# First batch of an attention kernel: softmax rows left unscaled, columns scaled after the value product

## Chip, cores and metric

The kernel runs on one core of one Trainium2 chip. The metric is device time in microseconds of one execution, as the median of several runs. The engines are TensorE (PE, with its weight loads PEld), VectorE (DVE), ScalarE (ACT), GpSimd (POOL) and SyncE (SP), which issues all DMA transfers of this kernel.

## The reference, cut to what matters

Attention with a memory part, over B = 4 batches, H = 8 heads, S = 576 tokens, D = 64, followed by two gated layers:

```python
a = np.exp(scores - scores.max(-1, keepdims=True))      # causal, scale 1/sqrt(D)
a /= a.sum(-1, keepdims=True) + 1e-09
local = np.matmul(a, v)
mem_out = (phi(q) @ M_prev) / (phi(q) @ z_prev + 1e-06)  # per row
g = 1.0 / (1.0 + np.exp(-beta))                          # per head
attn = g * mem_out + (1 - g) * local
x = attn as (2304, 512)
x = (sigmoid(x @ w_gate) * (x @ w_val)) @ w_out          # first layer, d_ff 1536
x = (h * clip(h + 3, 0, 6) / 6) @ w_out2, h = x @ w_in   # second layer, d_ff 2048
```

All of it is float32. In attention the products are float32 matmuls; in the layers each operand is split into a high and a low part and a product is three matmuls.

## The kernel before, in words

The program has three phases. Phase A does attention and, between its pieces, the first six of twelve feature blocks of the first layer; B does the rest of the first layer, C the second. Only A bears on the change.

Attention goes in 32 **visits** (`VISITS`, numbered v = 0 to 31). One visit is a pair of heads of one batch and one of two ranges of query rows: `rg` 0 is the first 320 tokens, `rg` 1 the other 256. The order is by batch, so visits 0 to 3 (`rg` 0) and 4 to 7 (`rg` 1) are the first batch. A visit takes two steps t of the loop in `phase_a`.

In a visit, TensorE makes scores (tile `s`, L344). DVE takes them from PSUM, adds the mask, writes them to tile `P` and keeps each row's minimum of the negated score (`m`, the custom instruction of L324; a row's first pass covers up to 320 or 448 columns, and for long rows a second pass of 256 or less). ACT takes the exponential in place and sums each row into `l` (L362). `normalize` then makes 1 / ((l + 1e-9) (1 + e^beta)) on DVE (L385, L386) and multiplies each row of `P` by it, on ACT (L390) in steps 5 to 26 and for the longest rows, else on DVE (L392). The first 64 columns of each row of `P` hold the memory part, phi(q) times `nr`, which `memory_rows` puts there on POOL (L377); `nr` comes from `prep_phi` (L297 to L309), which starts from the tile `aux` that a DMA brings. Three steps later TensorE transposes `P` in banks of four blocks (tile `t`, L402), ACT copies them to SBUF (`T`, L404), and `pv` multiplies by the memory matrix and the values (L426), ACT copies the product to `xpr` (L435), and SP stores it to DRAM (L438 to L442).

While the attention runs, weights of the layers are loaded as 64-bit values (`wst`, two 512 KB transfers each, L142) and **converted** by ACT and DVE to high and low halves: ACT L152, DVE L153, L154, L155, then ACT L163 and DVE L157, L158, L164. Nine such conversions of two blocks each lie in the first 117 us; the tile `wst` has two buffers, so a load waits for the conversion two before it. The first layer's matmuls (`m`, L233 to L235) come in between attention's pieces as soon as a stretch of 312 tokens has its attention; the first of them stand behind the value product of visit 4.

TensorE's order is the order in which the code is written (`manual_schedule`). The orders of DVE, ACT, POOL and SP are set by the scheduler of the framework, when the program is built, by its own estimate of times; each engine then works through its list in that order. PSUM tiles: `s` and `m` share four buffers (`ps_m`, tag `m`), `t` has three, `pv` one. The tile `aux` has three buffers, so the load for visit v + 3 waits for the value product of visit v.

Of the kernel before, what the change touches and what calls it, by code (L numbers as in the profile page):

```python
# [8 lines left out]
F32 = mybir.dt.float32  # L9
# [4 lines left out]
ALU = mybir.AluOpType  # L14
# [16 lines left out]
RANGES = [(0, 1, 2), (3, 4)]  # L31
# [15 lines left out]
NW_A = 3 * NFA // 2  # L47
NW_B = 3 * (FF1 - NFA) // 2
NLATE = 2

FILL = (5, 9, 8, 9, 8, 8)

# [26 lines left out]
class Kernel:  # L79
# [232 lines left out]
    def new_weights(self, v, rg):  # L312
        vs, nb = self.visits[v], len(ROWS[rg])
        vs["P", rg] = self.pa2.tile([128, 2304], F32, name="P", tag="P", bufs=3)
        vs["l", rg] = self.pa2.tile([128, 5], F32, name="l", tag="l")[:, :nb]
        vs["m", rg] = self.pa2.tile([128, 5], F32, name="m", tag="m")[:, :nb]

    def row(self, v, rg, r, a, e):
# [58 lines left out]
        self.nc.gpsimd.tensor_tensor(out, ph, nr, op=ALU.mult)  # L377

    def normalize(self, v, rg, act):
        nc = self.nc  # L380
        pr = self.visits[v]
        h = pr["pair"][1]
        l, nb = pr["l", rg], len(ROWS[rg])
        c0 = 5 * (h // 2) + 5 - nb
        nc.vector.scalar_tensor_tensor(l, l, 1e-9, self.a1[:, c0 : c0 + nb], op0=ALU.add, op1=ALU.mult)  # L385
        nc.vector.reciprocal(l, l)  # L386
        for r in range(nb):
            a = self.row(v, rg, r, 64, row_at(rg, r)[1])
            if act or row_at(rg, r)[1] == 640:
                nc.scalar.activation(a, a, AF.Copy, scale=l[:, r : r + 1])  # L390
            else:
                nc.vector.tensor_scalar_mul(a, a, l[:, r : r + 1])  # L392

    def transpose_bank(self, v, rg, k):
        nc = self.nc
        pr = self.visits[v]
        if k == 0:
            pr["T", rg] = self.pa2.tile([128, 2304], F32, name="T", tag="T")
        ps = self.ps_t.tile([128, 512], F32, name="t", tag="t")
        bank = BANKS[rg][k]  # L400
        for n, (r, j) in enumerate(bank):
            nc.tensor.transpose(ps[:, 128 * n : 128 * n + 128], self.row(v, rg, r, 128 * j, 128 * j + 128), self.ident)  # L402
        c = 128 * len(bank)
        nc.scalar.copy(pr["T", rg][:, 512 * k : 512 * k + c], ps[:, :c])  # L404

    def pv(self, v, rg):
        nc = self.nc
        pr = self.visits[v]
        b, h = pr["pair"]
        t0, nt = RTOK[rg]  # L410
        ps = self.ps_v.tile([128, 512], F32, name="pv", tag="pv")
        ops, T = [], pr["T", rg]
        for g in range(2):
            if rg == 0:

                o = 64 * g
                mine = [(0, 0, 320 * g, 320), (1, o, 640 + 256 * g, 256), (2, o + 128, 1152 + 128 * g, 128)]
            else:
                mine = [(j, 0, 1152 * g + 256 * j, 256) for j in range(4)] + [(4, 128, 1152 * g + 1024, 128)]
            ops.append(mine)  # L420
        last = len(ops[0]) - 1
        for n in range(last + 1):
            for g in range(2):
                j, o, c, w = ops[g][n]
                rows = slice(64 * g, 64 * g + 64)
                nc.tensor.matmul(  # L426
                    ps[rows, o : o + w],
                    pr["v"][:, j, rows],
                    T[:, c : c + w],
                    start=(n == 0),  # L430
                    stop=(n == last),
                    skip_group_check=True,
                )
        x = self.pa2.tile([128, 320], F32, name="xpr", tag="xpr")
        nc.scalar.copy(x[:, :nt], ps[:, :nt])  # L435
        dst = self.xd[h // 2, :, b * S + t0 : b * S + t0 + nt]
        if rg == 0:
            nc.sync.dma_start(dst[64:], x[64:, :nt])  # L438
            nc.sync.dma_start(dst[:64, 64:], x[:64, : nt - 64])
            nc.sync.dma_start(dst[:64, :64], x[:64, nt - 64 : nt])  # L440
        else:
            nc.sync.dma_start(dst, x[:, :nt])  # L442
        if h == H - 2:
            self.done[b, rg] = self.step
# [63 lines left out]
    def phase_a(self):  # L508
        nc, tc = self.nc, self.tc
# [8 lines left out]
        nt = len(steps)  # L518
        self.xnext = None
        stream, c = None, 0  # L520
# [30 lines left out]
        t = self.step = 0  # L551
# [5 lines left out]
        while t < nt or tq or vq:  # L557
            self.step = t
            fill = FILL[max(c - 1, 0)]
            first = w = 0  # L560
            if t < nt:
                v, rg, i = steps[t]
                if i == UNITS[rg][0][-1]:
                    self.new_weights(v, rg)
                w = 64 + 128 * i
                first = w if w <= 512 else 320
                self.score_part(v, i, 0, first)
            if t == 0:
                self.prep_phi(0)
            if t < nt and i == RANGES[rg][-1]:  # L570
                self.memory_rows(v, rg)
            transposes(t, 2)
            if vq and vq[0][0] <= t:
                self.pv(*vq.pop(0)[1])
            if first < w or (tq and tq[0][0] <= t):
                moe(fill // 2)
                fill -= fill // 2
                if first < w:
                    self.score_part(v, i, first, w)
                transposes(t, 1)  # L580
            if t < nt:
                self.exponentials(v, i)
                if i == RANGES[rg][-1]:
                    self.normalize(v, rg, 5 <= t < 27)
                    tq += [(t + 3, (v, rg, j)) for j in range(len(BANKS[rg]))]
            moe(fill)
            if t < nt and i == UNITS[rg][0][-1]:
                self.load_visit(v + 2)
            if t < nt and i == RANGES[rg][-1]:
                self.prep_phi(v + 1)  # L590
            if t >= 5 and t % 2:
                self.w_convert()
            if len(self.wstaged) < 2:
                self.w_load()
            t += 1
# [6 lines left out]
        self.bx = self.pool(ctx, "bx", 1)  # L602
        self.wpool2 = self.pool(ctx, "wslots2", NW_B - NLATE)
        self.ps_g = self.pool(ctx, "ps_g", 4, space=PSUM)
# [6 lines left out]
        self.plan_weights(keys, [])  # L611
        self.wpools = [self.wpool2] * (NW_B - NLATE)
        for _ in range(2):
            self.w_load()
        n = 0
        while c < NCA or stream is not None:
            self.step += 1
            moe(8)
            if n < NW_B - NLATE - 2:
                self.w_next()  # L620
# [4 lines left out]
        self.br = self.pool(self.b_ctx, "br", 1, side="right")  # L625
        self.wpool3 = self.pool(self.b_ctx, "wslots3", NLATE)
        self.wpools += [self.wpool3] * NLATE + [self.wpool] * 2 * NPAIR
        self.ps_a = self.pool(ctx, "ps_a", 4, space=PSUM)
# [345 lines left out]
```

## Time and profile before

| | before |
|---|---|
| median of 3 runs | 1067.75 us (1067.61 to 1069.07) |
| the profiled execution: its time | 1067.68 us |
| the profiled execution: span in the trace | 1065.9 us |
| PE busy | 1029.6 us (97%) |
| DVE busy | 645.5 us (61%) |
| ACT busy | 550.8 us (52%) |
| POOL busy | 83.5 us (8%) |

The time is 1.8 us more than the span: what lies around it. Shares are of the whole span; the first 80 us, in which the first layer has no work yet, look quite different from the rest. TensorE's granted clock is 0.997 of full speed on the mean.

### The profile page before, as it was taken

How to read it: one execution, taken by the hardware profiler on the slowest of the kernel's cores; microseconds unless marked ns; L12 is line 12 of the kernel's file. 1: busy time of each engine (PE TensorE's matmuls, PEld its weight loads, DVE VectorE, ACT ScalarE, POOL GpSimd, SP SyncE). 2: the span in 40 equal slices, each digit the busy share in tenths (PEclk: the TensorE clock that was granted, in tenths of full speed). 3: DMA queues.
4: the chain of work that ended last, by engine and by line, in shares of the span. 5: the costliest groups of instructions: out<-in, count | busy, mean ns of one | idle time of the engine just before them, and what ended most of it. 6: DMA issues, size and time to landing. Idle time of an engine off the chain costs nothing.

```text
span 1065.9 us, 16031 instructions
## 1 busy us (share of the span) xinstructions
PE 1029.6 (97%) x5824; PEld 886.0 (83%) x5824; DVE 645.5 (61%) x1543; ACT 550.8 (52%) x1191; POOL 83.5 (8%) x102
## 2 busy tenths in 40 slices
PE   5689999999999999999999999999999999999998
PEld 3367678878887899999888888888888888888886
DVE  6989755454455438888888888743454433643432
ACT  5999875576556644435444343433453333633432
POOL 3212211110111000000000000310002000000000
PEclk9999999999999999999999999999999999999999
DMA  7756542424242215336686877444404542044511
GB/s 227 215 177 198 189 126 75 137 80 123 68 125 79 62 47 179 119 119 250 231 295 246 310 261 275 152 158 188 148 30 158 217 155 103 10 164 172 218 40 60
DMA packets 66239, 164.87 MB, mean 155 GB/s; under 512 B 8432, under 2 KB 41712, under 8 KB 60272
## 3 DMA queue, kind: packets, MB, share of 16 engines
q1 hardware_dynamic: 66160, 163.85, 44.8%
q8 instruction: 46, 0.75, 0.3%
q14 instruction: 33, 0.27, 0.1%
HBM read 122.76 MB, written 41.06 MB: 154 GB/s over the span
## 4 chain that ended last, share of the span: by engine, by line
PE 84%; DVE 5%; ACT 5%; DMA 4%; issue 1%; SPq 1%; POOL 1%; ACTq 0%; POOLq 0%; DVEq 0%
PE acc L822 18%; PE pa L787 9%; PE pb L787 7%; PE m L233 6%; PE m L234 5%; PE m L235 5%; PE g L235 5%; PE g L233 5%; PE g L234 5%; PE pv L426 4%; PE t L402 4%; PE s L344 3%; PE acc L234 2%; PE acc L235 2%; PE acc L233 2%; DMA aux<-in_aux 1%
## 5 line engine op out<-in xcount | busy, mean ns | idle before, releaser
L822 PE MATMUL acc<-wslot,hs 128*128 128x512 f32 x864 | 227.8, 395 | 2.2 <-ACT hs L228 2.2
L822 PEld LDWEIGHTS acc<-wslot,hs 128*128 128x128 f32 x864 | 159.5, 188 | 27.7 <-ACT hs L228 3.5
L787 PE MATMUL pa<-xq,wslot 128*128 128x384 f32 x576 | 117.3, 338 | 1.1 <-ACT u L887 0.6
L787 PEld LDWEIGHTS pa<-xq,wslot 128*128 128x128 f32 x576 | 103.7, 187 | 9.9 <-ACT u L887 0.9
L235 PE MATMUL g<-xs,wslot 128*128 128x468 f32 (+1 forms) x288 | 106.4, 370 | 0.0
L234 PE MATMUL g<-xs,wslot 128*128 128x468 f32 (+1 forms) x288 | 106.2, 369 | 0.0
L233 PE MATMUL g<-xs,wslot 128*128 128x468 f32 (+1 forms) x288 | 104.1, 369 | 0.0
L362 ACT ACTIVATE P<-P,m 128x192 f32<-128x192 f32 (+4 forms) x144 | 83.9, 584 | 31.1 <-DVE m L324 29.8
L233 PE MATMUL m<-xs,wslot 128*128 128x312 f32 x288 | 93.8, 326 | 0.3 <-DVE m L324 0.3
L234 PE MATMUL m<-xs,wslot 128*128 128x312 f32 x288 | 88.1, 306 | 0.0
L235 PE MATMUL m<-xs,wslot 128*128 128x312 f32 x288 | 87.9, 305 | 0.0
L787 PE MATMUL pb<-xq,wslot 128*128 128x384 f32 x432 | 87.8, 338 | 0.0
L787 PEld LDWEIGHTS pb<-xq,wslot 128*128 128x128 f32 x432 | 77.9, 188 | 6.3
L344 PE MATMUL s<-qk 64*128 64x320 f32 (+3 forms) x320 | 67.9, 494 | 13.6 <-DMA qk<-in_qk 10.8
L851 DVE TENSOR_TENSOR c<-pb,u 128x384 f32<-128x384 f32 x48 | 26.6, 555 | 87.0 <-ACT u L887 86.0
L799 ACT ACTIVATE r<-c,three 128x384 f32<-128x384 f32 x72 | 44.2, 613 | 63.0 <-DVE c L851 63.0
L402 PEld LDWEIGHTS t<-ident,P 128*128 128x128 f32 x464 | 52.8, 143 | 25.1 <-issue 14.9
L402 PE MATMUL t<-ident,P 128*128 128x128 f32 x464 | 67.2, 281 | 5.6 <-ACT T L404 2.7
L229 DVE TENSOR_TENSOR hs<-r,hs 128x384 fp32r<-128x384 f32 x96 | 55.8, 585 | 26.8 <-ACT hs L228 25.4
L324 DVE CUSTOM_DVE_ANT_0 P<-s,mask 128x320 f32<-128x320 f32 (+3 forms) x144 | 62.5, 452 | 12.9 <-PE s L344 12.5
L404 ACT COPY T<-t 128x512 f32<-128x512 f32 (+2 forms) x128 | 65.6, 540 | 8.8 <-PE t L402 8.7
L426 PE MATMUL pv<-T,aux 128*64 128x256 f32 (+2 forms) x512 | 61.3, 367 | 8.3 <-ACT T L404 8.3
(101 smaller groups left out, 1918.4 us busy)
## 6 DMA issues: line engine op xcount, KB each, us to landing
wst<-in_wm SPq DMA_DIRECT2D x68, 512.0 KB, 5.7
wslot<-wd SPq DMA_DIRECT2D x30, 1024.0 KB, 5.1
wd<-wslot SPq DMA_DIRECT2D x16, 1024.0 KB, 4.8
wslot<-wd SPq DMA_DIRECT2D x15, 768.0 KB, 6.2
wd<-wslot SPq DMA_DIRECT2D x8, 768.0 KB, 5.6
qk<-in_qk SPq DMA_DIRECT2D x32, 160.0 KB, 2.4
aux<-in_aux SPq DMA_DIRECT2D x16, 320.0 KB, 3.3
qk<-in_qk SPq DMA_DIRECT2D x16, 288.0 KB, 3.0
```

The costliest lines, as they stand in the source:

```text
L229: elo.tensor_tensor(lo, src, hi.bitcast(F32), op=ALU.subtract)
L233: nc.tensor.matmul(out, w[0], x[0], start=first, stop=False)
L234: nc.tensor.matmul(out, w[0], x[1], start=False, stop=False)
L235: nc.tensor.matmul(out, w[1], x[0], start=False, stop=last)
L324: self.nc.vector.tensor_tensor_reduce(out=self.row(v, rg, r, 64 + a, 64 + e), in0=ps, in1=mask, scale=-0.125, scalar=3.0e38 if a == 0 else ...
L344: nc.tensor.matmul(ps[:, : e - a], qk[rows, 0, q0 : q0 + 128], qk[rows, 1, a:e], start=True, stop=True)
L362: self.nc.scalar.activation(x, x, AF.Exp, bias=vs["m", rg][:, r : r + 1], scale=-1.0, accum_out=vs["l", rg][:, r : r + 1])
L402: nc.tensor.transpose(ps[:, 128 * n : 128 * n + 128], self.row(v, rg, r, 128 * j, 128 * j + 128), self.ident)
L404: nc.scalar.copy(pr["T", rg][:, 512 * k : 512 * k + c], ps[:, :c])
L426: nc.tensor.matmul(ps[rows, o : o + w], pr["v"][:, j, rows], T[:, c : c + w], start=(n == 0), stop=(n == last), skip_group_check=True,)
L787: nc.tensor.matmul(ps[:, :HC], w[:, i, b, cc], x[:, l, k], start=first and k == 0 and n == 0, stop=last and k == 1 and n == 2, skip_group_ ...
L822: nc.tensor.matmul(a, h[:, i, cc], w[:, l, f], start=first and f == 0 and n == 0, stop=last and f == 1 and n == 2)
```

## The change

For visits 0 to 7 (`POST = 8`), `normalize` no longer scales the rows of `P`. With f = (l + 1e-9)(1 + e^beta) for a row, it multiplies `nr` by f, so that the memory columns of `P` carry the same factor as the unscaled exponentials, and makes 1 / f. `memory_rows` is called after `normalize` for these visits, since it needs the new `nr`; before, it stood behind the scores. Behind the value product, `spread` turns 1 / f, which lies over partitions, into a PSUM tile `rl` with the factors along columns, the same in all 64 partitions of a head: a matmul of `l`'s column, repeated 64 times, with the identity. There are six such matmuls for `rg` 0, four for `rg` 1; the tile is one of the four of `ps_m`. DVE then multiplies `xpr` by `rl` before it is stored. The tile `l` gets four buffers.

```diff
+POST = 8
...
-        vs["l", rg] = self.pa2.tile([128, 5], F32, name="l", tag="l")[:, :nb]
+        vs["l", rg] = self.pa2.tile([128, 5], F32, name="l", tag="l", bufs=4)[:, :nb]
...
         nc.vector.scalar_tensor_tensor(l, l, 1e-9, self.a1[:, c0 : c0 + nb], op0=ALU.add, op1=ALU.mult)
+        if v < POST:
+            nc.vector.tensor_tensor(pr["nr"], pr["nr"], l, op=ALU.mult)
+            nc.vector.reciprocal(l, l)
+            return
         nc.vector.reciprocal(l, l)
...
+    def spread(self, v, rg):
+        l = self.visits[v]["l", rg]
+        ps = self.ps_m.tile([128, 512], F32, name="rl", tag="m")
+        if rg == 0:
+            cols = [[(1, 0, 0, 128), (2, 128, 0, 128), (0, 256, 0, 64)], [(0, 0, 64, 64), (3, 64, 0, 128), (4, 192, 0, 128)]]
+        else:
+            cols = [[(2 * g + n, 128 * n, 0, 128) for n in range(2)] for g in range(2)]
+        for n in range(len(cols[0])):
+            for g in range(2):
+                r, o, c, w = cols[g][n]
+                nc.tensor.matmul(
+                    ps[64 * g : 64 * g + 64, o : o + w],
+                    l[:, r : r + 1].to_broadcast([128, 64]),
+                    self.ident[:, c : c + w],
...
+        return ps
...
         nc.scalar.copy(x[:, :nt], ps[:, :nt])
+        if v < POST:
+            nc.vector.tensor_tensor(x[:, :nt], x[:, :nt], self.spread(v, rg)[:, :nt], op=ALU.mult)
...
-            if t < nt and i == RANGES[rg][-1]:
+            if t < nt and i == RANGES[rg][-1] and v >= POST:
                 self.memory_rows(v, rg)
...
                     self.normalize(v, rg, 5 <= t < 27)
+                    if v < POST:
+                        self.memory_rows(v, rg)
```

The lists of the engines show what else moves. Of a row's names, `P_517`/`P_522` and `l_518`/`l_523` belong to visit 5, `P_608`/`P_618` to visit 6; line numbers of the change are two or more higher from L315 on.

On TensorE, at the end of visit 3's value product (`pv_559`, `pv_563`), before:

```order
L426 MATMUL pv_559<-T_526,aux_213 64x320 x2
L426 MATMUL pv_559<-T_526,aux_213 64x256 x2
L426 MATMUL pv_559<-T_526,aux_213 64x128 x2
L344 MATMUL s_571<-qk_369 128x256
L344 MATMUL s_573<-qk_369 128x256
L344 MATMUL s_611<-qk_455 128x448
L344 MATMUL s_613<-qk_455 128x448
L402 MATMUL t_618<-ident_95,P_426 128x128 x4
```

and with the change:

```order
L456 MATMUL pv_563<-T_531,aux_209 64x128 x2
L426 MATMUL rl_572<-ident_95,l_333 64x128
L426 MATMUL rl_572<-ident_95,l_333 64x64
L426 MATMUL rl_572<-ident_95,l_333 64x128 x2
L426 MATMUL rl_572<-ident_95,l_333 64x64
L426 MATMUL rl_572<-ident_95,l_333 64x128
L346 MATMUL s_583<-qk_365 128x256
L346 MATMUL s_585<-qk_365 128x256
L346 MATMUL s_621<-qk_455 128x448
L346 MATMUL s_623<-qk_455 128x448
L410 MATMUL t_628<-ident_95,P_426 128x128 x4
```

The matmuls of `spread` stand between the value product and the next scores; apart from such pieces (24 rows of the list for eight visits) TensorE's list is the same.

On DVE, at the passes over visit 5's last 256 columns (second score tiles of `P_517`), before; `wst_333` is the third weight conversion:

```order
L155 SCALAR_TENSOR_TENSOR wst_333<-wst_333,wf_505 128x1024
L309 RECIPROCAL nr_405<-nr_405 128x4
L386 RECIPROCAL l_427<-l_427 128x4
L157 TENSOR_SCALAR wf_505<-wst_333 128x1024
L299 SCALAR_TENSOR_TENSOR ph_494<-aux_370,phw_495 128x256
L324 ISA P_517,m_519<-s_571,mask_100,m_519 128x256
L324 ISA m_519 128x1
L158 ISA wst_333<-wst_333,wf_505 128x1024x2
L324 ISA P_517,m_519<-s_573,mask_100,m_519 128x256
L324 ISA m_519 128x1
L306 TENSOR_REDUCE nr_496<-phw_495 128x4
L324 ISA P_608,m_610<-s_611,mask_100 128x448
```

and with the change, where `wst_423` is the fourth conversion and the third has ended eleven rows above:

```order
L326 ISA P_522,m_524<-s_559,mask_100 128x320
L326 ISA m_524 128x1
L159 TENSOR_SCALAR wf_606<-wst_423 128x1024
L310 SCALAR_TENSOR_TENSOR nr_501<-nr_501,a2_109 128x4
L160 ISA wst_423<-wst_423,wf_606 128x1024x2
L311 RECIPROCAL nr_501<-nr_501 128x4
L166 TENSOR_TENSOR wslot_605<-wst_423,wslot_605 128x1024
L467 TENSOR_TENSOR xpr_570<-xpr_570,rl_572 128x320
L299 TENSOR_SCALAR phw_596<-aux_456 128x256
L326 ISA P_522,m_524<-s_583,mask_100,m_524 128x256
L326 ISA m_524 128x1
L155 TENSOR_SCALAR wf_717<-wf_717 128x1024
```

The rest of the third conversion and all of the fourth, and the product with visit 3's factors (`xpr_570`), have moved ahead of these passes.

Further down on DVE with the change, up to the product that visit 5's memory rows need (`nr_501` by `l_523`); `wst_519` is the fifth conversion:

```order
L156 TENSOR_SCALAR wf_717<-wf_717 128x1024
L389 SCALAR_TENSOR_TENSOR l_523<-l_523,a1_108 128x4
L326 ISA P_618,m_620<-s_678,mask_100 128x320
L326 ISA m_620 128x1
L308 TENSOR_REDUCE nr_597<-phw_596 128x4
L326 ISA P_618,m_620<-s_680,mask_100 128x320
L326 ISA m_620 128x1
L157 SCALAR_TENSOR_TENSOR wst_519<-wst_519,wf_717 128x1024
L391 TENSOR_TENSOR nr_501<-nr_501,l_523 128x4
```

Before, POOL's product for the same visit needed only L309 of `nr_496`, which did not wait for visit 5's exponentials; now it stands behind them and behind a part of the fifth conversion.

## Rows read from the trace of the kernel before

**Rows 1.** Busy time of the engines by stretch: us, busy of each, clock, DMA

```profile
20.00:40.00 20.00, 14.42 (x96) 7.91 (x94) 19.26 (x65) 18.93 (x52) 5.72 (x7) 1.00 0.66 179
40.00:60.00 20.00, 14.36 (x87) 8.13 (x87) 19.59 (x58) 20.00 (x43) 4.95 (x6) 0.91 0.71 234
60.00:80.00 20.00, 17.21 (x122) 13.35 (x118) 15.88 (x39) 19.53 (x45) 1.78 (x3) 1.00 0.55 168
```

**Rows 2.** Waits of PE from 13 to 82 us: total, times, longest

```profile
PE pv L426 <- ACT T L404: 5.8, 6, 2.2
PE s L344 <- DVE m L324: 2.8, 2, 2.6
PE t L402 <- ACT T L404: 2.5, 1, 2.5
```

**Rows 3.** Groups by line, 0 to 82 us: total busy us, mean ns | idle before

```profile
L390 ACT ACTIVATE P<-P,l 128x448 f32<-128x448 f32 (+4 forms) x26 | 14.2, 635 | 0.0
...
L158 DVE CUSTOM_DVE_ANT_0 wst<-wst,wf 128x2048 uint16<-128x2048 uint16 x6 | 7.6, 1272 | 0.0
L377 POOL TENSOR_TENSOR P<-ph,nr 128x320 f32<-128x320 f32 (+1 forms) x8 | 7.4, 926 | 29.8 <-DVE nr L309 25.1 <-DVE l L386 4.7
L155 DVE SCALAR_TENSOR_TENSOR wst<-wst,wf 128x1024 int32<-128x1024 int32 x6 | 7.4, 1228 | 0.0
...
L164 DVE TENSOR_TENSOR wslot<-wst,wslot 128x1024 fp32r<-128x1024 f32 x5 | 6.2, 1237 | 0.0
L154 DVE TENSOR_SCALAR wf<-wf 128x1024 int32<-128x1024 int32 x6 | 4.4, 735 | 0.0
L157 DVE TENSOR_SCALAR wf<-wst 128x1024 int32<-128x1024 uint32 x6 | 4.1, 686 | 0.0
L153 DVE TENSOR_SCALAR wf<-wf 128x1024 f32<-128x1024 f32 x6 | 4.1, 682 | 2.7 <-ACT wf L152 2.7
L392 DVE TENSOR_SCALAR P<-P,l 128x192 f32<-128x192 f32 (+2 forms) x10 | 3.2, 384 | 0.0
...
L488 DVE SCALAR_TENSOR_TENSOR th<-th,m 128x312 f32<-128x312 f32 x2 | 0.9, 473 | 0.0
```

**Rows 4.** DVE in order of time: start us, us, instruction [idle before <-releaser]

```profile
13.83 0.69 DVE L153 TENSOR_SCALAR wf<-wf 128x1024 f32<-128x1024 f32 x1 [0.99 <-ACT wf L152]
...
46.95 0.48 DVE L324 CUSTOM_DVE_ANT_0 P<-s,mask,m 128x256 f32<-128x256 f32 x1
...
47.35 1.35 DVE L158 CUSTOM_DVE_ANT_0 wst<-wst,wf 128x2048 uint16<-128x2048 uint16 x1
...
49.89 1.23 DVE L164 TENSOR_TENSOR wslot<-wst,wslot 128x1024 fp32r<-128x1024 f32 x1
...
66.84 0.29 DVE L297 TENSOR_SCALAR phw<-aux 128x256 f32<-128x256 f32 x1 [1.41 <-DMA aux<-in_aux]
...
67.65 0.48 DVE L324 CUSTOM_DVE_ANT_0 P<-s,mask 128x320 f32<-128x320 f32 x1
```

**Rows 5.** PE in order of time, transposes of visit 5 to visit 8

```profile
57.30 0.99 PE L402 MATMUL t<-ident,P 128*128 128x128 f32 x7 [0.23 <-ACT P L390]
...
60.31 0.41 PE L233 MATMUL m<-xs,wslot 128*128 128x312 f32 x1
...
68.20 1.11 PE L344 MATMUL s<-qk 64*128 64x256 f32 x4 [2.61 <-DVE m L324]
...
70.72 0.59 PE L344 MATMUL s<-qk 64*128 64x192 f32 x2
...
73.29 2.17 PE L426 MATMUL pv<-T,aux 128*64 128x256 f32 x20
```

**Rows 6.** The chain that ended last: visit 7's `aux` load, start us and us

```profile
63.21 3.60 DMA aux<-in_aux
```

**Rows 7.** PE in order of time, value product of visit 11

```profile
131.23 1.90 PE L426 MATMUL pv<-T,aux 128*64 128x320 f32 x10 [2.24 <-ACT T L404]
```

**Rows 8.** Busy time of the engines by stretch, as in group 1

```profile
132.00:134.00 2.00, 2.00 (x8) 1.39 (x6) 0.42 (x1) 0.43 (x1) 0.00 (x0) 0.50 0.00 0
```

More of the change, by code (lines that the diff above doesn't have):

```diff
@@ L404, in transpose_bank @@
         nc.scalar.copy(pr["T", rg][:, 512 * k : 512 * k + c], ps[:, :c])
+    def spread(self, v, rg):
+        nc = self.nc
+        l = self.visits[v]["l", rg]
[11 more added lines that the diff above has]
+                    self.ident[:, c : c + w],
+                    start=True,
+                    stop=True,
+                    skip_group_check=True,
+                )
+        return ps
     def pv(self, v, rg):
```

## Prediction

> **What bounds the kernel now.** Over the whole span TensorE is the bound: 97% busy. Since its list only grows by the change, a gain can come only from its idle time, and I first looked where that lies. The stretches by engine answer it [rows 1]: from 20 to 80 us PE is busy 14.4, 14.4 and 17.2 us in each 20, while DVE is busy 19.3, 19.6 and 15.9 and ACT 18.9, 20.0 and 19.5. So until about 80 us two engines are saturated side by side, DVE to 63 us, ACT a little longer, and PE follows them. Its waits in this part [rows 2] name ACT's copies of the transposes (5.8 and 2.5 us) and DVE's row passes (2.8 us). The reader is to see that "waits for ACT" is no proof that ACT alone is the bound: an engine that works through its list in order, and whose exponentials wait for DVE's row passes, passes DVE's lateness on under its own name.
>
> **What it removes.** In the first batch the scaling of `P`: on ACT 26 instructions of 14.2 us together, on DVE ten of 3.2 us [rows 3]. ACT becomes clearly lighter. DVE does not: it gets, for each of eight visits, the product of `xpr` with `rl`. No row shows it; the nearest is the product of a PSUM tile and an SBUF tile of 312 columns at L488, 0.47 us [rows 3]. An instruction holds the engine some 0.08 us less than its row says, as the next one starts before its end (46.95 plus 0.48 against 47.35 [rows 4]). So about 0.4 us each, 3.2 us for eight, bounded by 0.3 and 0.6; and eight products of a few columns, some 0.1 us each, bounded by nothing and 0.2. DVE's total comes out 0.8 us higher.
>
> **What it adds on TensorE.** Four or six matmuls of at most 128 columns for a visit, in two halves of the array. Such a pair costs what a part of the value product does: eight of 256 and two of 128 columns take 2.17 us [rows 5], in pairs; in proportion to columns 0.24 us for a pair of 128. That is 0.48 us for a visit of the second range and 0.6 to 0.7 for one of the first. Visits 0 to 4 have theirs while PE waits anyway; those of visits 5, 6 and 7 fall behind 70 us, where PE hardly waits: 3 x 0.48 = 1.4 us on the path. The bounds are 0.8 and 2.
>
> **What it moves.** This is the larger part. The lists in the section on the change show that the scheduler fills DVE's list differently: weight conversions have moved forward. One conversion is six DVE instructions, 5.84 us by their means [rows 3], or 5.3 without the overlaps. Before, at the first pass over visit 5's last 256 columns, two conversions and four sixths of the third are done; now the rest of the third (L158 and L164, 2.3 us) and the whole fourth (5.3) are ahead of it. The sum of DVE's work between the first conversion's start (13.83) and this pass (46.95 [rows 4]) changes thus: 2.3 + 5.3 for conversions, four products with `rl` 1.6, five with `nr` 0.5, about 1 for small steps of `prep_phi` and a split that moved ahead too (an estimate, each below the 0.47 of L488's row), less 1.5 for visit 1's scaling, half of the ten rows of L392. That is 9.2 us more. Idle time of DVE can take little of it: between 20 and 60 us it is busy 38.85 of 40 us [rows 1], so 1.2 us at most, and somewhat more if instructions that were stretched by a neighbour run freely. Hence the pass starts at about 46.95 + 9.2 - 1.2 = 55.0, bounds 53.8 and 57.
>
> Queued behind it on DVE is the new product of `nr` and `l` for visit 5, another 5.7 us of list: five row passes, one L155, two of L153's kind, small steps. So it is done near 60.8; POOL's product takes 0.93 [rows 3], and TensorE can transpose visit 5 at 61.7 instead of 57.30 [rows 5]. Behind those transposes stand visit 4's value product and the first matmuls of the layer, which move from 60.31 to about 64.7, with their own `rl` to 65.2. That PE is late here costs nothing by itself, since it waits 2.61 us at 68.20 [rows 5]. But the value product of visit 4 frees the `aux` buffer of visit 7. That load takes 3.60 us [rows 6]; before, it was issued at 63.21 and DVE stood at L297 until 66.84 [rows 4]. Now SP can issue it at about 65.1, it lands near 69.0, and visit 7's next row pass stands further behind L297 (products, two conversion steps and one of `prep_phi`, 2.2 us, instead of 0.8): 71.3 instead of 67.65 [rows 4]. The scores at 68.20 wait for the buffer which that pass frees. So they move by 3.6 us; some 0.6 us is covered, because the tile of `spread` frees a buffer a little sooner than the score tile does. I take 3.0 us for PE's lateness at visit 8 (70.72 [rows 5]); bounds: 1.2 if DVE never waits in between, 5.5 if it waits as much as it did before and TensorE's clock falls once more in this part (below).
>
> From there PE is the bound again, and DVE, whose conversions now lie behind it, gets ahead of the old times. ACT's saving is worth nothing there.
>
> **A stall further on.** In visit 11's value product PE waits 2.24 us [rows 7], and the granted clock is then 0.50, the lower of its levels, 1.2 GHz [rows 8], which costs nearly 2 us more. ACT's copy stood behind work that waited for an `aux` load. With the change the weight loads that delayed it come earlier. But the copy of the last bank stays behind visit 12's scaling, which is unchanged. I take 1.0 us off; bounds: nothing and 4.2.
>
> **Sum.** 3.0 + 1.4 - 1.0 = 3.4 us on a profiled execution of 1067.68, which is the median of the runs shown within 0.1 us: 1071.1 us. A change under 0.2% (2.1 us) can't be told from none with this kernel.
>
> **A rule against the trace.** The rows say that DVE had less than 1.2 us of idle time in 40 [rows 1], beside ACT. The Trainium skill ("Perfetto Trace Analysis", section Optimization Strategies) says that where the matmul engine idles for others, one should optimize those that block it; the waits' view names ACT, so by that rule the change gains. By the rows of the waits that gain would be the third rival below; by the sum of DVE's list it is none. Whoever leaves out this page loses no term.
>
> **Rivals.**
> First, the same time: PE's lateness at visit 8 stays near its lower bound, 1.2 us, and the stall at 131 us goes, clock and all: 1.2 + 1.4 - 4.2 = -1.6, or with half of the stall gone +0.5. 1067 to 1069 us. For it: DVE's list after 90 us is shorter than before, PE comes later and its suppliers don't. Against it: visit 12's scaling still stands ahead of the copy.
> Second, slower by more: `rl` is one of four buffers that scores and layer matmuls share, and it is held until DVE comes to its product, which stands behind conversions. From 70 to 105 us DVE's list then ties PE down as well, and each `aux` load waits for a later value product. Two or three waits of 1 us each and one more fall of the clock give 1074 to 1076. It decides if DVE reaches visit 9's row passes more than 4 us later than before.
> Third, faster: ACT was the bound, DVE merely kept busy by conversions that nobody needed yet, and PE loses its waits for ACT (5.8 + 2.5 [rows 2]) less the 1.4 of new matmuls: 1060.8 us; with half of it 1064. It needs DVE's row passes of visits 5 and 6 to come no later than before, against the 9.2 us of work that stand ahead of them. The page's rule has its chance here.
>
> **Chances.** Slower by 1 to 6 us as summed: 0.55, with a range of its own from 1069 to 1073.5; same time by the first rival 0.23; much slower 0.12; faster 0.10. Of the forecast's 0.55 about 0.06 lies within 2.1 us. So faster by over 0.2% 0.10, within 0.2% 0.29, slower 0.61. The range from 1066.3 to 1074.8 leaves out most of the faster cases and a third of the much slower ones, together about 0.15.
>
> **What would show it.** Right: DVE's pass over visit 5's last columns at 53.8 to 57 us, with four conversions (L164) ended before it; visit 5's first transposes later than 60 us, released by POOL; the first layer matmul at 64 to 66; PE at visit 8's scores at 72 to 76; ACT with idle time between 40 and 80 us, where it had none; the waits of PE there put down to DVE and POOL in place of ACT. Wrong: if visit 5's last passes are at 47 to 50 us, the step on moved conversions fails, and with it the sign; if they are late but visit 8's scores come at 71 us, something regains what I take as lost, most likely the `aux` load; if both are late and the time is the same, it was regained at the stall at 131 us. If one group of `rl` takes over 0.8 us on PE, the new matmuls are mis-sized.

## The result, and the profile of the changed kernel

| | before | changed |
|---|---|---|
| median of four runs | 1067.99 us | 1075.83 us (1073.87 to 1076.9) |
| the profiled execution | 1067.68 us | 1073.87 us |
| its span | 1065.9 us | 1072.1 us |
| PE busy | 1029.6 us | 1038.5 us |
| DVE busy | 645.5 us | 649.1 us |
| ACT busy | 550.8 us | 539.5 us |

The change makes the kernel slower: ratio 1.0062, 95% interval 1.0045 to 1.0079 (the quotient of the two medians, 1.0073, lies inside it). On the time shown before, the ratio gives 1074.4 us. The forecast was 1071.1: the sign is right, and the size about half of what came. The time lies in the stated range (1066.3 to 1074.8), near its upper end, and above the 1069 to 1073.5 that the forecast case had for itself. The profiled execution is the fastest of the four, so that its trace has 6.2 us to explain, less than the medians differ by.

The stretches from 20 to 80 us, which answer to [rows 1]: busy time of PE, PEld, DVE, ACT and POOL, then the granted clock.

```profile
20.00:40.00 20.00, 17.56 (x131) 12.30 (x130) 19.11 (x58) 15.49 (x43) 4.33 (x6) 0.91 0.73 229
40.00:60.00 20.00, 11.87 (x56) 6.66 (x54) 19.07 (x52) 11.79 (x24) 4.96 (x5) 0.81 0.51 168
60.00:80.00 20.00, 18.82 (x130) 13.59 (x130) 17.47 (x52) 16.45 (x38) 2.10 (x4) 0.94 0.62 190
```

ACT has become the lighter engine (15.5, 11.8 and 16.5 us of 20 instead of 18.9, 20.0 and 19.5). DVE is as full as before, and PE loses its time between 40 and 60 us, at a lower clock too. The waits of PE from 13 to 82 us, which answer to [rows 2]:

```profile
PE s L346 <- DMA qk<-in_qk: 5.9, 1, 5.9
PE t L410 <- POOL P L379: 5.6, 2, 4.6
PE s L346 <- DVE xpr L467: 2.6, 1, 2.6
PE pv L456 <- ACT T L412: 2.4, 2, 1.9
PE s L346 <- DVE m L326: 1.6, 3, 0.9
```

The first row, a wait for the first loads, was there before too (6.4 us). Of the others POOL and DVE have taken the place of ACT, as forecast; before, PE waited 1.7 us for POOL (neither of these two rows of before stands in [rows 2]). The longest of these waits, 4.6 us, is at a place that the prediction did not look at. PE in order of time, for [rows 5]:

```profile
45.27 2.49 PE L410 MATMUL t<-ident,P 128*128 128x128 f32 x11 [4.63 <-POOL P L379]
...
56.89 1.86 PE L346 MATMUL s<-qk 64*128 64x448 f32 x2 [2.61 <-DVE xpr L467]
58.68 2.82 PE L410 MATMUL t<-ident,P 128*128 128x128 f32 x12
...
66.05 1.09 PE L410 MATMUL t<-ident,P 128*128 128x128 f32 x8 [0.95 <-POOL P L379]
67.07 2.17 PE L456 MATMUL pv<-T,aux 128*64 128x256 f32 x20
69.07 0.61 PE L426 MATMUL rl<-ident,l 128*64 128x128 f32 x8
69.60 0.41 PE L235 MATMUL m<-xs,wslot 128*128 128x312 f32 x1
...
77.48 1.00 PE L346 MATMUL s<-qk 64*128 64x192 f32 x4 [0.20 <-DVE m L326]
...
97.86 0.80 PE L346 MATMUL s<-qk 64*128 64x320 f32 x2 [1.24 <-DVE xpr L467]
...
140.04 0.86 PE L456 MATMUL pv<-T,aux 128*64 128x256 f32 x6 [1.42 <-ACT T L412]
```

The first row is visit 3: its transposes wait for POOL's memory rows. Visit 5's transposes follow at 66.05, the first layer matmul at 69.60, and visit 8's scores at 77.48, 6.8 us later than before. Two signs of the prediction are thus missed (64 to 66 for the layer, 72 to 76 for visit 8). The two waits for `xpr` are score tiles whose buffer a tile of `spread` still holds. The last row is visit 11's value product, the place of [rows 7]. DVE in order of time, which answers to [rows 4]:

```profile
37.63 0.68 DVE L156 TENSOR_SCALAR wf<-wf 128x1024 int32<-128x1024 int32 x1
...
40.17 1.22 DVE L157 SCALAR_TENSOR_TENSOR wst<-wst,wf 128x1024 int32<-128x1024 int32 x1
...
41.71 0.18 DVE L311 RECIPROCAL nr<-nr 128x5 f32<-128x5 f32 x1
...
44.20 0.16 DVE L391 TENSOR_TENSOR nr<-nr,l 128x5 f32<-128x5 f32 x1
...
55.21 1.23 DVE L166 TENSOR_TENSOR wslot<-wst,wslot 128x1024 fp32r<-128x1024 f32 x1
56.35 0.48 DVE L467 TENSOR_TENSOR xpr<-xpr,rl 128x320 f32<-128x320 f32 x1
...
56.95 0.48 DVE L326 CUSTOM_DVE_ANT_0 P<-s,mask,m 128x256 f32<-128x256 f32 x1
...
61.21 0.17 DVE L389 SCALAR_TENSOR_TENSOR l<-l,a 128x4 f32<-128x4 f32 x1 [0.53 <-ACT P L364]
62.79 0.49 DVE L326 CUSTOM_DVE_ANT_0 P<-s,mask 128x320 f32<-128x320 f32 x1 [1.41 <-PE s L346]
...
65.08 0.16 DVE L391 TENSOR_TENSOR nr<-nr,l 128x4 f32<-128x4 f32 x1
...
73.70 0.48 DVE L326 CUSTOM_DVE_ANT_0 P<-s,mask 128x320 f32<-128x320 f32 x1
```

L166 ends the fourth conversion; the first pass over visit 5's last columns stands behind it at 56.95. The rows from 61.21 on lead to the product for visit 5's memory rows (65.08) and to visit 7's first row pass (73.70); on this way DVE waits for ACT and for PE. Further up, the third conversion (L156, L157) already stands ahead of visit 3's `nr` (L311) and of its product with `l` (L391). Before, that reciprocal ran at 36.18, and visit 3's rows and transposes followed at 36.51 and 39.40 (rows of before that were not shown above):

```profile
36.18 0.18 DVE L309 RECIPROCAL nr<-nr 128x5 f32<-128x5 f32 x1
```

```profile
36.51 0.79 POOL L377 TENSOR_TENSOR P<-ph,nr 128x320 f32<-128x320 f32 x1 [3.18 <-DVE nr L309]
```

```profile
39.40 1.42 PE L402 MATMUL t<-ident,P 128*128 128x128 f32 x11
```

The stall of [rows 7] has become shorter: the wait in visit 11's value product is now at 140.04 and takes 1.42 us instead of 2.24. The granted clock behind it stays at 1.00, where it was 0.50 and then 0.65 before. First the changed kernel in four stretches, then the one of before that follows on [rows 8]:

```profile
44.00:49.00 5.00, 3.73 (x15) 2.60 (x15) 4.13 (x10) 3.14 (x8) 0.72 (x1) 0.66 0.13 34
...
56.00:60.00 4.00, 3.11 (x8) 1.82 (x9) 4.00 (x14) 1.73 (x5) 0.59 (x1) 0.50 0.58 180
...
140.00:142.00 2.00, 1.96 (x14) 1.46 (x14) 0.13 (x1) 0.85 (x2) 0.00 (x0) 1.00 0.03 6
142.00:144.00 2.00, 2.00 (x14) 1.49 (x14) 1.10 (x5) 0.85 (x4) 0.00 (x0) 1.00 0.87 244
```

```profile
134.00:136.00 2.00, 2.00 (x9) 1.34 (x9) 0.13 (x1) 0.43 (x1) 0.00 (x0) 0.65 0.84 219
```

### The profile page after: what moved, and what is told of

Same layout as the page of the kernel before. It is cut to its first block, busy times and chain, and to the rows that moved or that the text cites. A ratio compares the mean times of both kernels' runs of the same rounds, so it can differ in the third digit from the quotient of the medians.

```text
span 1072.1 us, 16183 instructions
## 1 busy us (share of the span) xinstructions
PE 1038.5 (97%) x5904; PEld 894.4 (83%) x5904; DVE 649.1 (61%) x1549; ACT 539.5 (50%) x1165; POOL 82.9 (8%) x102
## 4 chain that ended last, share of the span: by engine, by line
PE 87%; DVE 4%; DMA 3%; ACT 3%; SPq 1%; issue 1%; POOL 0%; ACTq 0%; DVEq 0%
PE acc L856 18%; PE pa L821 9%; PE pb L821 7%; PE m L235 6%; PE g L237 6%; PE g L235 6%; PE g L236 6%; PE m L236 5%; PE m L237 5%; PE pv L456 4%; PE t L410 4%; PE s L346 4%; PE acc L235 3%; PE acc L237 3%; PE acc L236 3%; DMA xc<-xd 1%
## 5 line engine op out<-in xcount | busy, mean ns | idle before, releaser
L346 PE MATMUL s<-qk 64*128 64x320 f32 (+3 forms) x320 | 71.7, 497 | 15.8 <-DMA qk<-in_qk 10.3
L154 ACT ACTIVATE wf<-wst 128x512 f32<-128x512 f32 (+1 forms) x59 | 44.1, 747 | 44.9 <-DVE wst L160 38.7
```

The costliest lines, as they stand in the source:

```text
L346: nc.tensor.matmul(ps[:, : e - a], qk[rows, 0, q0 : q0 + 128], qk[rows, 1, a:e], start=True, stop=True)
```

## The experiments

Three theories stood at the start. A: the order on DVE, with conversions moved ahead. B: the tile of `spread` holds one of the four score buffers. C: the memory rows wait for the row sums. The table has every run, five rounds each beside the kernel before (the changed kernel has the four runs of the result), with four places in its trace: POOL's memory rows of visit 3, DVE's first pass over visit 5's last columns, PE's scores of visit 8 and of visit 16, the first of the third batch (all us). A trace is one execution, and the times of one kernel spread by several us (hold: 1066.1 to 1074.2), so that small differences between the last columns mean little. rows_early, no_spread, only_unscaled and scaled_and_spread leave a factor out or apply it twice, as their expectations say; their times alone are of use.

| kernel | ratio, 95% interval | rows v3 | pass v5 | scores v8 | scores v16 |
|---|---|---|---|---|---|
| before | 1 | 36.51 | 46.95 | 70.72 | 156.46 |
| changed | 1.0062 [1.0045, 1.0079] | 44.50 | 56.95 | 77.48 | 163.17 |
| hold | 1.0009 [0.9993, 1.0025] | 38.57 | 48.62 | 69.36 | 160.11 |
| h11 | 1.0061 [1.0049, 1.0073] | 44.96 | 56.40 | 77.03 | 163.26 |
| before_ahead | 1.0106 [1.0087, 1.0125] | 35.71 | 61.99 | 83.91 | 168.26 |
| rl_in_t | 1.0038 [1.0027, 1.0050] | 45.01 | 57.29 | 77.05 | 162.40 |
| rows_early | 1.0041 [1.0028, 1.0054] | 43.11 | 54.81 | 79.42 | 163.16 |
| no_spread | 1.0044 [1.0029, 1.0059] | 45.02 | 55.17 | 78.64 | 161.34 |
| only_unscaled | 0.9996 [0.9987, 1.0006] | 41.98 | 52.99 | 71.28 | 155.68 |
| scaled_and_spread | 1.0039 [1.0025, 1.0053] | 38.27 | 48.16 | 73.89 | 161.92 |
| hold_rlt | 1.0016 [1.0003, 1.0029] | 40.47 | 51.12 | 72.00 | 161.32 |
| pool_product | 1.0055 [1.0037, 1.0074] | 43.35 | 50.45 | 78.55 | 165.58 |
| pool_hold | 1.0005 [0.9992, 1.0019] | 38.76 | 49.68 | 71.11 | 157.41 |
| post4_hold | 1.0034 [1.0021, 1.0046] | 38.29 | 48.63 | 70.65 | 161.48 |

**The order alone, undone (hold).**

```diff
-        self.nc.vector.tensor_tensor_reduce(
+        self.last = self.nc.vector.tensor_tensor_reduce(
...
             if t >= 5 and t % 2:
-                self.w_convert()
+                if t in (9, 11):
+                    with tc.issue_after(self.last.ins):
+                        self.w_convert()
+                else:
+                    self.w_convert()
```

> The change, with the third and fourth weight conversions tied on DVE's list behind the last row pass of their own step (issue order only), so that two conversions stand ahead of visit 5's last passes, as before, and the third behind them. A (the conversions moved ahead are the cause): visit 5's last passes near 50 us instead of 57, visit 8's scores at 71.5 to 74 instead of 77.5, time 1068.5 to 1071.5. B (the tile of spread holds a score buffer) or C (memory rows behind the normalization): visit 8's scores stay at 76 to 78 and the time at 1073.5 to 1077.

It came as A said, and more: the pass at 48.62, visit 8's scores at 69.36 (A had 71.5 to 74), ratio 1.0009. With the change's other parts in place, tying two conversions takes off 0.53% of its 0.62%. Visit 3's transposes no longer wait, but further on PE loses time again (PE in order of time):

```profile
39.35 1.42 PE L410 MATMUL t<-ident,P 128*128 128x128 f32 x11
...
90.18 0.80 PE L346 MATMUL s<-qk 64*128 64x320 f32 x2 [1.38 <-DVE th L520]
...
135.13 2.44 PE L456 MATMUL pv<-T,aux 128*64 128x320 f32 x10 [2.59 <-ACT T L412]
```

DVE, with the conversions that were put off, is busy 19.5 us from 80 to 100 us (19.2 before), PE waits for it until 90.18, and the stall of the kernel before is back at 135.13. So visit 8 is 1.4 us early and visit 16 is 3.7 us late.

**The order alone, made (before_ahead).** The kernel before, with the fourth conversion put ahead of visit 5's last passes and visit 6's first passes kept behind these.

```diff
+                if t == 11:
+                    self.w_convert()
+                    with tc.issue_after(self.last.ins):
+                        self.score_part(v, i, first, w)
+                elif first < w:
-                if first < w:
                     self.score_part(v, i, first, w)
```

Here `self.last` is the last instruction of the conversion; the same form keeps the scores of step 12 behind the pass, and the conversion at the end of step 11 is left out.

> The kernel before, with nothing of the change except the order on DVE: the rest of the third and the whole fourth weight conversion are put ahead of visit 5's last passes (issue order only; visit 6's first passes stay behind these, and the sixth conversion comes ahead of visit 7's last passes too). A (the moved conversions are the cause): visit 5's last passes at 53 to 56 us instead of 47, visit 8's scores at 74 to 78 instead of 70.7, time 1071.5 to 1076. If the order costs nothing by itself and the lateness comes from spread, its tile or the memory rows: visit 8's scores at 70 to 72.5 and 1067 to 1069.5.

It is slower by 1.06%, more than the change, with nothing else of it. PE in order of time:

```profile
62.53 1.83 PE L344 MATMUL s<-qk 64*128 64x320 f32 x4 [12.85 <-DVE m L324]
```

A's order of events came, later than A had it: the pass at 61.99 and not at 53 to 56, in part because DVE also waited 3.9 us for ACT's part of a split of `xc` (L229) that had moved ahead with the conversions. What is shown is that conversions ahead of these passes can by themselves cost more than the change does. It is not the change's order, and that the change's own order does so by itself is not shown; only_unscaled, below, speaks against it.

**One conversion tied, not two (h11).** As hold, with `t in (11,)`: only the fourth stays behind.

> The change, with only the fourth weight conversion tied behind the row passes of its own step: three conversions stand ahead of visit 5's last passes (before two and four sixths, in the change four). A, with lateness in proportion to the work ahead: visit 8's scores at 71.5 to 74, and the time between the one with both tied and the change, 1069.5 to 1072. If what the tied conversions cost behind visit 8 (the stall near 131 us, waits near 90) is a price of tying both, this one keeps the gain at 131 us and comes to 1067.5 to 1069.5.

Both expectations missed: it is as slow as the change. DVE in order of time, and a part of the chain that ended last (start us, us, what), show why:

```profile
56.19 0.29 DVE L299 TENSOR_SCALAR phw<-aux 128x256 f32<-128x256 f32 x1 [3.49 <-DMA aux<-in_aux]
56.40 0.48 DVE L326 CUSTOM_DVE_ANT_0 P<-s,mask,m 128x256 f32<-128x256 f32 x1
```

```profile
44.96 0.73 POOL P L379
...
45.74 2.36 PE t L410 x11
...
49.47 1.57 PE pv L456 x7
...
51.59 4.57 DMA aux<-in_aux
...
56.19 0.31 DVE phw L299
```

With the fourth conversion out of the way, DVE waits 3.49 us in front of the same pass, for the `aux` of visit 6. The chain leads from there to visit 3's value product, whose end frees the buffer, to its transposes, and to its rows on POOL, which are at 44.96 as late as in the change. Two paths of nearly equal length lead to visit 5's last passes: the conversions in DVE's list, and visit 3's late rows by way of the `aux` load. Undoing one uncovers the other; hold, which ties the third conversion too, undoes both.

**The memory rows (rows_early).** `memory_rows` called where it was, from the unchanged `nr`, so that the product of `nr` with `l` goes.

> The change, with the memory rows written as before, from the unchanged nr and not behind the normalization (the factor of a row's sum is left out of the memory columns); spread and its product stay. C (the transposes wait for POOL, which now waits for the row sums): the 4.6 us wait of visit 3's transposes and the low clock behind it go, visit 8's scores come at 71 to 74 and the time is 1068.5 to 1071.5. A: conversions still stand ahead (three and two thirds instead of four before visit 5's last passes), so visit 8's scores at 75 to 77.5 and 1072.5 to 1076.

The time (median 1072.87) is what A said; visit 8's scores, at 79.42, are later than either theory had them. POOL's row of visit 3 still comes at 43.11, though nothing of the row sums stands before it:

```profile
43.11 0.72 POOL L379 TENSOR_TENSOR P<-ph,nr 128x320 f32<-128x320 f32 x1 [6.26 <-DVE nr L311]
```

It waits for the plain `nr`, whose small steps stand behind the moved conversion. By this run the wait for the row sums accounts for 1.4 of the 8.0 us by which visit 3's rows are late (44.50 against 43.11). By the trace of the change itself it is 2.5: there the plain `nr` is 5.5 us late (41.71 against 36.18), and here 6.6. So for visit 3's rows C is the smaller part. For the time it is not ruled out; no_spread, below, bears on that.

**The buffer of `spread` (rl_in_t, hold_rlt).** The tile is taken from the transposes' pool:

```diff
-        ps = self.ps_m.tile([128, 512], F32, name="rl", tag="m")
+        ps = self.ps_t.tile([128, 512], F32, name="rl", tag="t")
```

> The change, with the tile of spread in the three buffers of the transposes instead of the four of the scores; the lists of DVE and TensorE are otherwise the same. A: only the waits of the scores for the product with rl go (2.6 us at 57 us, which is covered, and 1.2 us at 98 us): 1074 to 1075.5, visit 8's scores still at 76 to 78. B: visit 8's scores at 72 to 74.5, time 1069.5 to 1072. A rival to both: the transposes now wait for the product instead, and the time stays at 1075 to 1078.

> Both edits that helped: the third and fourth conversions tied behind the row passes of their own step, and the tile of spread in the transposes' buffers. If the two add up (5.6 and 2.6 us off the change's time): 1066 to 1068, just below before. If they heal the same lateness: 1068 to 1070.5, as with the order alone, with the stall near 131 us still there.

Alone it gives 1.0038 where the change has 1.0062; the time lies between the two expectations, and the intervals overlap, so that the 0.24% are likely but not settled. Visit 8's scores stay at 77.05, as A said: B is at most a part of the cost. The rival came in part too, as the transposes now wait 3.1 us for the product, in three waits. On top of hold the edit gains nothing (1.0016 against 1.0009).

**Parts of the change (only_unscaled, scaled_and_spread, no_spread).** The first leaves out `spread`, the product and the late rows; the second keeps the scaling and adds `spread` and the product; the third leaves out `spread` and the product alone:

```diff
-        if v < POST:
-            nc.vector.tensor_tensor(x[:, :nt], x[:, :nt], self.spread(v, rg)[:, :nt], op=ALU.mult)
```

> Only ACT's and DVE's saving: the rows of the first eight visits stay unscaled, and nothing is put in its place (no spread, no product, memory rows as before; the factors are left out of the result). ACT as the bound (third rival of the prediction): PE loses most of its waits before 80 us and the time is 1060 to 1063.5. DVE as the bound: before visit 8's scores little is gained (they come at 69.5 to 72), the stall at 131 us goes, 1063.5 to 1066.5. If the time stays at 1067 to 1069, the saving is worth nothing and everything that the change costs is the price of what it adds.

> The opposite half of the change: rows scaled and memory rows written as before, and spread and its product added on top (the columns are scaled twice). Two conversions and three sixths stand ahead of visit 5's last passes, nearly as before. A: the new matmuls cost 1.4 to 2 us on the path and the product 3 us of DVE's list, so visit 8's scores at 71.5 to 74 and 1069.5 to 1072. B (the tile holds a score buffer): waits of the scores for xpr of 1 to 3 us and 1072 to 1076.

> The change without spread and its product (the columns stay unscaled); memory rows behind the normalization, and all four conversions ahead of visit 5's last passes, as in the change. A and C: visit 8's scores at 73.5 to 76.5, no 1.2 us wait near 98 us and no rl on the path, 1069.5 to 1073. B and the added work (matmuls, products) as the main cause: visit 8's scores at 70 to 73 and 1066.5 to 1069.

only_unscaled takes ACT's 14.2 us away, with nothing in its place, and the time stays where it was (0.9996). The Trainium skill ("Perfetto Trace Analysis", section Optimization Strategies) advises, where the matmul engine waits for others, to optimize the engines that block the critical path. Here the waits named ACT, and this saving is worth at most 0.13%, the lower end of the interval. But it does not relieve ACT alone: the scheduler moves the conversions forward here too. Visit 3's rows come 5.5 us late, visit 5's pass 6.0 us late, and PE waits at visit 3's transposes (PE of only_unscaled, then of no_spread):

```profile
42.76 2.61 PE L409 MATMUL t<-ident,P 128*128 128x128 f32 x11 [5.53 <-POOL P L379]
```

```profile
45.80 2.61 PE L410 MATMUL t<-ident,P 128*128 128x128 f32 x11 [8.56 <-POOL P L379]
```

Yet visit 8's scores are only 0.6 us late in only_unscaled. So this lateness before 57 us does not by itself cost time. Four of the kernels leave the order to the scheduler and differ in two parts. With neither part (only_unscaled) the ratio is 0.9996; with `spread` and its product (rows_early) 1.0041; with the late memory rows (no_spread) 1.0044; with both (the change) 1.0062. Each part alone brings about 0.45%, clear of the intervals, also C's part, by which visit 3's rows come 3.0 us later (45.02 against 41.98). In the two kernels with late rows the last two steps of the fourth conversion are also ahead of visit 5's pass, so that C stands here for late rows with the list that they bring.

In no_spread the time is within A's and C's range, but visit 8 (78.64) is later than said and later than in the change; the waits for `xpr` and the new matmuls are missing, and by visit 16 it has 1.8 us on the change. scaled_and_spread came as A said (73.89, median 1072.15): what it adds costs 0.39% where the rows are scaled and the order is nearly kept. There visit 5's transposes wait 3.73 us for POOL. In hold the new parts cost less than that, with ACT lighter and visit 8 early.

**Ways out (pool_product, pool_hold, post4_hold).** In the first two ACT copies `rl` to SBUF and POOL multiplies; the second ties the conversions as hold does; the third is hold with `POST = 4`.

```diff
-            nc.vector.tensor_tensor(x[:, :nt], x[:, :nt], self.spread(v, rg)[:, :nt], op=ALU.mult)
+            y = self.pa2.tile([128, 320], F32, name="rls", tag="rls")
+            nc.scalar.copy(y[:, :nt], self.spread(v, rg)[:, :nt])
+            nc.gpsimd.tensor_tensor(x[:, :nt], x[:, :nt], y[:, :nt], op=ALU.mult)
```

> The change, with the product with rl taken off DVE: ACT, which has become lighter, copies the tile of spread to SBUF and POOL multiplies. DVE's list loses eight products of about 0.4 us and the score buffer is freed by ACT; the scheduler puts three conversions and one sixth ahead of visit 5's last passes. A: visit 8's scores at 72 to 75.5, time 1069.5 to 1072.5. If POOL's lateness now delays the stores and the first layer's input: first layer matmul after 70 us and 1073 to 1077.

> The product on POOL by way of ACT, and the third and fourth conversions tied behind the row passes of their own step. A: visit 8's scores at 68.5 to 70.5; DVE has 3 us less to do by 90 us than with the tie alone, so the conversions that were put off come earlier and the waits between 85 and 135 us shrink: 1066 to 1069, no slower than before. If the new matmuls, the later memory rows and the clock are what is left: 1069 to 1071, as with the tie alone.

> The change for visits 0 to 3 alone (the others are scaled on ACT and have early memory rows, as before), with the third and fourth conversions tied behind the row passes of their own step. The matmuls of spread on the path (1.5 us) go, and visits 4 to 7 don't wait for POOL behind the row sums. A, if the lists are then close to those of before: 1066.5 to 1069, within 0.1% of before. If the time is 1070 or more, the cost lies in the first four visits, that is in the order of DVE before 50 us.

Taking the product off DVE gives nothing while the order stays free, and A missed: visit 5's pass comes earlier than in the change (50.45), but PE then waits 5.34 us for POOL's rows at visit 5's transposes; the time (median 1075.27) is that of its rival. With the order tied it has the lowest ratio of the versions with the whole change (1.0005), not to be told from the kernel before, nor from hold; visit 8's scores (71.11) are a little later than A had them. `POST = 4` with the tie missed its expectation. Its loss does not lie in the first four visits, as visit 8's scores are on time at 70.65; it comes later, where the layer needs weights whose conversion was put off (PE in order of time):

```profile
118.31 0.41 PE L235 MATMUL m<-ha,wslot 128*128 128x312 f32 x1 [2.54 <-ACT wslot L165]
...
121.62 0.63 PE L237 MATMUL m<-ha,wslot 128*128 128x312 f32 x1 [2.75 <-DVE wslot L166]
```

No version beats the kernel before.

## Why the prediction was right in its sign and too low in its size

- **What bounds the kernel**: that ACT's saving would not make the kernel faster is right, and the third rival (faster by 3.7 us or more) falls by the result and by only_unscaled. That DVE and not ACT bounds PE up to 80 us is not shown: only_unscaled moves DVE's order as well, and only_unscaled with the order tied was not run. In hold, where ACT is lighter and the order tied, visit 8 is 1.4 us early.
- **DVE's total, and the new products**: DVE is busy 3.6 us longer over the whole kernel (649.1 against 645.5), not 0.8. Where the other 2.8 us come from was not followed up; the place of the passes came out right without them.
- **The moved conversions ahead of visit 5's last passes**: right, 56.95 within 53.8 to 57 (2.0 us above the 55.0 taken), and the four conversions ended before it.
- **From there to visit 8's scores, the 3.0 us**: the mis-sized term. It measured 6.8 us, beyond the upper bound of 5.5. The step that failed is "another 5.7 us of list" from the pass to the product of `nr` and `l`: it took 8.1 us (56.95 to 65.08). DVE did not only work through its list there; it waited 0.53 us for ACT and 1.41 us for PE's scores of visit 6, 1.9 of the 2.4 us. These scores were late because PE had waited 2.61 us for the score buffer at 56.89 and then ran at a clock of 0.50. So visit 5's transposes came at 66.05 and not at 61.7. The `aux` load then took 2.07 us and not 3.60 (the prediction's own 65.1 and 3.60 make 68.7, not the 69.0 that it went on with), and still visit 7's first pass came 6.0 us late (73.70 against 67.65) and not 3.6. From there PE lost another 0.7 us, where the prediction had taken 0.6 as covered. The buffer's wait does not explain it alone: in rl_in_t, without it, the same step takes 6.0 us, and visit 8 is still at 77.05.
- **What the sum left out**: it began at visit 5. The third conversion, also moved ahead, was already in front of visit 3's `nr`, so that visit 3's rows came 8.0 us late and its transposes 5.9 us. "Visits 0 to 4 have theirs while PE waits anyway" speaks of the new matmuls, and for the rows of these visits the prediction had no term. h11 shows that this lateness, by way of the `aux` load of visit 6, can hold visit 5's pass at the same place without the fourth conversion; only_unscaled shows that a lateness of 5.5 us there need not reach visit 8. How much of the 6.8 us comes from it stays open. The clock was 0.66 and 0.50 of full speed in two stretches, where the prediction had put one such fall into the bound only.
- **The score buffer**: the second rival had named it. In the trace it is 2.61 us at 56.89 and 1.24 us at 97.86. The rival's time, 1074 to 1076, is what came, and so did its sign, as DVE reached visit 9's row passes 7.6 us later than before (90.88 against 83.27). But its mechanism was to work from 70 to 105 us, where only the second of these waits lies and the granted clock stays at 1.00; and with the buffer moved visit 8 is as late as in the change.
- **The matmuls of `spread`**: 69.07 to 69.60 is 0.53 us for a visit, against 0.48; three of them are 1.6 us against 1.4.
- **The stall near 131 us**: right that a part of the wait stays, and too small at the 1.0 taken. The trace gives 2.5 us: PE is 9.2 us late at the value products of visits 8 to 10 (109.33 against 100.10 for the first), and 6.7 us late at visit 16's scores. Of this 0.8 is the shorter wait (1.42 against 2.24), and about 1.7 the clock, which before stood at 0.50 and 0.65 for 2 us each (an estimate from these two rows). In hold, where the conversions come late again, the stall is back.

The sum in the order of the trace: 6.8 at visit 8, 1.6 for `spread` and 1.2 for the wait at 97.86, 0.4 regained between, 2.5 regained at the stall, 0.5 regained later: 6.2 us, the difference of the spans (1072.1 - 1065.9).

What the runs show of the cause: the cost goes almost wholly when two conversions are tied (hold), and none is left when `spread` and the late rows are out and the order stays moved (only_unscaled, with the saving still in). With the rows unscaled it is thus neither the order's alone nor that of the added parts alone, but comes where both meet (with the rows scaled, `spread` and its product cost 0.39% in nearly the old order). What stays open: by which of the paths the 6.8 us at visit 8 come about, how much of the change is the score buffer (rl_in_t, 0.24% with overlapping intervals), what the saving is worth with the order kept, and why hold_rlt is not better than hold.

## What to carry to other kernels

When a change makes inputs ready sooner for one engine, a scheduler that fills each engine's list by its own estimates may put unneeded bulk work ahead of small steps that the bottleneck waits for; look for the first place in the list where this happens, not only the one with the largest piece. Then test what it costs: here the moved order cost nothing that could be measured until other work was added to it. A tie in issue order on two bulk steps gave back 0.53% here without any change in the work. If undoing one cause gives nothing, look at what the engine waits for at the same place: two paths of equal length hide each other. When a stage is late, look for a stall of before at its new time: at the old time of this one the trace shows another piece of work.

## What was not expected of the hardware

After the 4.63 us wait at 45.27, visit 3's eleven transposes took 2.49 us, where hold's took 1.42 us without a wait; the granted clock of 44 to 49 us is 0.66, and behind the 2.61 us wait at 56.89 it is 0.50, that is 1.2 GHz. In hold the clock fell behind a wait of 1.38 us: PE was busy 0.80 us of the 2 us from 88 to 90, and from 92 to 94 the granted clock is 0.50. Behind the 1.42 us at 140.04 in the changed kernel it did not fall, so that the length of the wait alone does not decide it. Where the clock falls, the matmuls behind a wait take longer too; whether that reaches the end is another question, as in only_unscaled the eleven transposes behind a wait of 5.53 us took 2.61 us, with a granted clock of 0.74 from 40 to 60 us, and the time stayed the same. The two stretches of hold, in columns as above:

```profile
88.00:90.00 2.00, 0.80 (x3) 0.29 (x2) 2.00 (x4) 1.76 (x5) 0.00 (x0) 1.00 0.88 285
92.00:94.00 2.00, 2.00 (x10) 2.00 (x9) 2.00 (x5) 1.95 (x6) 0.55 (x1) 0.50 0.56 162
```
